# A six-layer cross network on one core: another way to load and transpose the last 32 features of x0

## The chip, the core and the metric

The kernel runs on one NeuronCore of a Trainium2 chip. The core has five instruction streams: TensorE (PE in the profile; PEld is its weight load), VectorE (DVE), ScalarE (ACT), GpSimd (POOL) and SyncE (SP, which only issues transfers here). ScalarE issues transfers too. A transfer (DMA) runs on the core's 16 DMA engines. The metric is device microseconds of one execution; shorter is better. Most executions of one kernel agree within 0.3%.

## The reference

x0 is 4096 x 416, ws is 6 x 416 x 416, bs is 6 x 416, all bfloat16.

```python
def reference(x0, ws, bs):
    x = x0
    for l in range(ws.shape[0]):
        x = x0 * (x @ ws[l] + bs[l]) + x
    return x
```

## The kernel before, in words

The 416 features are cut into NK = 3 groups of 128, the main part, and a remainder of R = 32. For layers 0 to 4 the activations lie transposed, features on partitions: `XM[i]` holds the main part (128 partitions, 3 groups, 4096 columns of batch), `XR[i]` the remainder. The batch is cut in NS = 2 halves of 2048 and each half in NG = 4 blocks of CW = 512. The remainder would fill only 32 partitions, so the four blocks of a half are stacked: partition 32g + r of `XR` is feature 384 + r of block g, and `XR` has 512 columns per half. `XM[0]` and `XR[0]` hold x0 and are read in every layer. `XRd` is a copy of `XR[0]` with its upper and lower 64 partitions exchanged; only layer 0 reads it.

**The loads.** `load_x0t(s, g)` (L75) loads one of the eight x0 blocks, main part, 512 rows, through a transposing DMA on SyncE's queue. `load_wm(eng, l)` (L71) loads a layer's main weights, `load_wr0` (L87) the remainder rows of layer 0's weights to 32 partitions of `WR`, which L108 (ScalarE, twice) and L110 (GpSimd) copy to the other three groups of 32. Layer 0's main weights, the biases (`bsb`, L100), the remainder of half 0 and `load_wr0` are issued by ScalarE in this order, followed by a dummy activation on `dz` (L104) that brings the load of the activation table with it. A transfer is also held back at its issue until the transfer that had its completion semaphore before has landed; there are eight such semaphores, given out in turn.

**The remainder of x0** reaches `XR[0]` in three steps. For half 0, `load_xrem0` (L80) issues four transfers on ScalarE's queue, each for every fourth tile of 128 rows, so that a row of `xrig[:, 0, i]` holds the 32 remainder features of four batch rows side by side. For half 1, `load_xrem1` (L84) is one transfer on SyncE's queue to `xrem`, after the fifth x0 block, and GpSimd (L132) rearranges `xrem` to `xrig[:, 1]`. Then `x0_rem(s, tpr)` (L153) transposes four 128x128 tiles on TensorE (L155) into PSUM, and VectorE copies the result to `XR[0]` and, in two exchanged halves, to `XRd` (L158).

**Layer 0** (`first_layer`, L206) runs half by half. `full` (L212) multiplies the three main groups of one block, `row` (L219) adds the remainder's product; for the output group m = 1 it reads `XRd`. `mm_rem` (L191, L196) makes the 32 remainder outputs. In half 0 the order on TensorE is: nine `full` matmuls of block 0, the four remainder transposes, nine of block 1, eight `row` matmuls, eighteen for blocks 2 and 3, four `row`, `mm_rem`, the four transposes for half 1. Each PSUM result goes through ScalarE, which adds the bias (L163, L171), and VectorE, which multiplies by x0 (L164, L172) and adds x (L167, L173). PSUM is a pool of four tiles of two banks each; the transposes of half 0 take a tile of their own, those of half 1 the second bank of the remainder tile `pr`.

**Layers 1 to 4** use the same parts with matmuls of 32 output columns (L179, L185), and the last layer works with batch on partitions (L325 to L353) and stores the output. While the first transfers are under way, TensorE runs filler matmuls (L139).

A scheduler orders the instructions of each engine by its own estimates; an instruction given to `tc.keep_in_program_order` keeps its place on its engine in the order of the program.

Of the kernel before, what the change touches and what calls it, by code (L numbers as in the profile page):

```python
# [9 lines left out]
ACT = mybir.ActivationFunctionType  # L10
ALU = mybir.AluOpType
BF16 = mybir.dt.bfloat16
# [4 lines left out]
def kernel(  # L17
# [7 lines left out]
    nc = tc.nc  # L25
    B, D = x0.shape
    L = ws.shape[0]
    P = 128
    NK = 3
    R = D - NK * P  # L30
    assert R == 32 and B == 4096 and D == 416 and L >= 2
    NS = 2
    NG = 4
    CW = 512
    SW = NG * CW
# [4 lines left out]
    big = ctx.enter_context(tc.tile_pool(name="big", bufs=1))  # L40
    tpool = ctx.enter_context(tc.tile_pool(name="tpool", bufs=6))
    opool = ctx.enter_context(tc.tile_pool(name="opool", bufs=10))
    psum = ctx.enter_context(tc.tile_pool(name="psum", bufs=4, space=bass.MemoryType.PSUM))

    x0_v = x0.rearrange("(bt p) d -> p bt d", p=P)
    out_v = out.rearrange("(bt p) d -> p bt d", p=P)

    ident = const.tile([P, P], BF16)
    dz = const.tile([P, 2], FP32)
    ones = const.tile([P, P], BF16)  # L50
    WM = const.tile([P, L, NK, D], BF16)
    WR = const.tile([P, L, D], BF16)
# [3 lines left out]
    bM = const.tile([P, NK, L], FP32)  # L56
    bR = const.tile([P, L], FP32)
    X0rows = big.tile([P, NBT, D], BF16)
    XLrows = big.tile([P, NBT, D], BF16)
    scrR = [big.tile([P, 4, P], BF16, name=f"scrR{s}") for s in range(NS)]  # L60
    xrem = big.tile([P, 16, R], BF16)
    xrig = big.tile([P, NS, 4, P], BF16)
    XRd = big.tile([P, NS * CW], BF16)
    XM = [big.tile([P, NK, B], BF16, name=f"XM{i}") for i in range(3)]
    XR = [big.tile([P, NS * CW], BF16, name=f"XR{i}") for i in range(3)]

    def col0(s, g):
        return SW * s + CW * g
# [4 lines left out]
    def load_x0t(s, g):  # L73
        c0 = col0(s, g)
        nc.sync.dma_start_transpose(out=XM[0][:, :, c0:c0 + CW], in_=x0[c0:c0 + CW, 0:NK * P])  # L75

    def load_xrem0():
        with nc.allow_non_contiguous_dma(reason="64B row segments"):
            for i in range(4):
                nc.scalar.dma_start(xrig[:, 0, i, :].rearrange("p (g r) -> p g r", g=NG), x0_v[:, i:16:4, NK * P:D])  # L80

    def load_xrem1():
        with nc.allow_non_contiguous_dma(reason="64B row segments"):
            nc.sync.dma_start(xrem[:], x0_v[:, 16:32, NK * P:D])  # L84

    def load_wr0():
        nc.scalar.dma_start(WR[0:R, 0, :], ws[0, NK * P:D, :])  # L87

    def load_wr(eng, g, l0, l1):
        eng.dma_start(WR[32 * g:32 * g + 32, l0:l1, :], ws[l0:l1, NK * P:D, :].rearrange("l r n -> r l n"))  # L90
# [8 lines left out]
    load_wm(nc.scalar, 0)  # L99
    nc.scalar.dma_start(bsb[:], bs[:, :])  # L100
    load_x0t(0, 1)
    load_xrem0()
    load_wr0()
    nc.scalar.activation(dz[:, 1:2], dz[:, 0:1], ACT.Identity, bias=dz[:, 0:1], scale=1.0)  # L104
    for g in range(1, NG):
        dst, src = WR[32 * g:32 * g + 32, 0, :], WR[0:R, 0, :]
        if g < NG - 1:
            nc.scalar.copy(dst, src)  # L108
        else:
            nc.gpsimd.tensor_copy(dst, src)  # L110
    for g in range(2, NG):
        load_x0t(0, g)
    load_x0t(1, 0)
    load_xrem1()
    for g in range(1, NG):
        load_x0t(1, g)
    load_wm(nc.sync, 1)
    for g in range(NG):
# [8 lines left out]
    def fill_wd(l0, l1):  # L127
        for g in range(NG):
            nc.gpsimd.tensor_copy(WD[32 * g:32 * g + 32, l0:l1, g, :], WR[32 * g:32 * g + 32, l0:l1, NK * P:D])

    fill_wd(0, 1)
    nc.gpsimd.tensor_copy(xrig[:, 1].rearrange("p i (g r) -> p i g r", g=NG), xrem[:].rearrange("p (g i) r -> p i g r", g=NG))  # L132
    fill_wd(1, L)

    wps = psum.tile([P, CW], FP32, tag="ps", name="wps")
# [8 lines left out]
    def bias_setup():  # L144
        pb = psum.tile([P, 4, 8], BF16, tag="ps", name="pb")
        for m in range(NK):
            nc.tensor.transpose(pb[:, m, 0:L], bsb[0:L, 128 * m:128 * m + 128], ident[0:L, 0:L])
        for g in range(NG):
            nc.tensor.transpose(pb[32 * g:32 * g + 32, 3, 0:L], bsb[0:L, NK * P:D], ident[0:L, 0:L], tile_position=(0, 32 * g))  # L149
        nc.vector.tensor_copy(bM[:], pb[:, 0:NK, 0:L])  # L150
        nc.vector.tensor_copy(bR[:], pb[:, 3, 0:L])

    def x0_rem(s, tpr):  # L153
        for i in range(4):
            nc.tensor.transpose(tpr[:, 128 * i:128 * i + 128], xrig[:, s, i, :], ident[:])  # L155
        for dst, src in ((slice(0, P), slice(0, P)), (slice(64, P), slice(0, 64)), (slice(0, 64), slice(64, P))):
            to = XR[0] if dst == src else XRd
            nc.vector.tensor_copy(to[dst, CW * s:CW * s + CW], tpr[src])  # L158

    def ew_main(l, s, m, h, pt, cur, nxt, pin=False):  # L160
        c0 = col0(s, 2 * h)
        t = tpool.tile([P, 2 * CW], BF16, name="t")
        nc.scalar.activation(t[:], pt[:].rearrange("p a b -> p (a b)"), ACT.Identity, bias=bM[:, m, l:l + 1], scale=1.0)  # L163
        prod = nc.vector.tensor_tensor(out=t[:], in0=t[:], in1=XM[0][:, m, c0:c0 + 2 * CW], op=ALU.mult)  # L164
        if pin:
            tc.keep_in_program_order(prod)
        nc.vector.tensor_tensor(out=nxt[:, m, c0:c0 + 2 * CW], in0=t[:], in1=cur[:, m, c0:c0 + 2 * CW], op=ALU.add)  # L167

    def ew_rem(l, s, pr, curR, nxtR):
        tr = tpool.tile([P, 2 * CW], BF16, name="t")  # L170
        nc.scalar.activation(tr[:, 0:CW], pr, ACT.Identity, bias=bR[:, l:l + 1], scale=1.0)  # L171
        nc.vector.tensor_tensor(out=tr[:, 0:CW], in0=tr[:, 0:CW], in1=XR[0][:, CW * s:CW * s + CW], op=ALU.mult)  # L172
        nc.vector.tensor_tensor(out=nxtR[:, CW * s:CW * s + CW], in0=tr[:, 0:CW], in1=curR[:, CW * s:CW * s + CW], op=ALU.add)  # L173
# [15 lines left out]
    def mm_rem(l, s, pr, cur, curR):  # L189
        for g in range(NG):  # L190
            nc.tensor.matmul(pr[32 * g:32 * g + 32, :], lhsT=WD[:, l, g, :], rhs=curR[:, CW * s:CW * s + CW],  # L191
                             start=True, stop=False, tile_position=(0, 32 * g))
        for k in range(NK):
            for g in range(NG):
                c0 = col0(s, g)
                nc.tensor.matmul(pr[32 * g:32 * g + 32, :], lhsT=WM[:, l, k, NK * P:D], rhs=cur[:, k, c0:c0 + CW],  # L196
                      start=False, stop=(k == NK - 1), tile_position=(0, 32 * g))
# [8 lines left out]
    def first_layer(s):  # L206
        cur, curR, nxt, nxtR = XM[0], XR[0], XM[1], XR[1]

        def full(pt, m, h, gl, after_row):
            c0 = col0(s, 2 * h + gl)  # L210
            for k in range(NK):
                nc.tensor.matmul(pt[:, gl, :], lhsT=WM[:, 0, k, 128 * m:128 * m + 128], rhs=cur[:, k, c0:c0 + CW],  # L212
                                 start=(k == 0 and not after_row), stop=(k == NK - 1 and after_row))

        def row(pt, m, h, opens):
            for gl in range(2):
                rg = 32 * ((2 * h + gl) ^ (2 if m == 1 else 0))
                src = XRd if m == 1 else curR
                nc.tensor.matmul(pt[:, gl, :], lhsT=WR[rg:rg + 32, 0, 128 * m:128 * m + 128],  # L219
                                 rhs=src[rg:rg + 32, CW * s:CW * s + CW],  # L220
                                 start=opens, stop=not opens, tile_position=(rg, 0))

        def ph(m):
            return psum.tile([P, 2, CW], FP32, tag="ps", name=f"ph{m}")

        pa = [ph(m) for m in range(NK)]
        if s == 0:
            for m in range(NK):
                full(pa[m], m, 0, 0, False)
            tp0 = psum.tile([P, CW], BF16, tag="ps", name="tpr")  # L230
            x0_rem(0, tp0[:])
            for m in range(NK):
                full(pa[m], m, 0, 1, False)
        else:
            for m in range(NK):
                for gl in range(2):
                    full(pa[m], m, 0, gl, False)
        pb = [ph(0)]
        row(pa[0], 0, 0, False)
        row(pb[0], 0, 1, True)  # L240
        row(pa[2], 2, 0, False)
        row(pa[1], 1, 0, False)
        for m in range(NK):
            ew_main(0, s, m, 0, pa[m], cur, nxt)
        for m in range(NK):
            if m:
                pb.append(ph(m))
            for gl in range(2):
                full(pb[m], m, 1, gl, m == 0)
        row(pb[1], 1, 1, False)  # L250
        row(pb[2], 2, 1, False)
        pr = psum.tile([P, 2, CW], FP32, tag="ps", name="pr")
        mm_rem(0, s, pr[:, 0, :], cur, curR)
        if s == 0:
            x0_rem(1, pr[:, 1, :].bitcast(BF16)[:, 0:CW])
        for m in range(NK):
            ew_main(0, s, m, 1, pb[m], cur, nxt, pin=(s == 0))
        ew_rem(0, s, pr[:, 0, :], curR, nxtR)

    bias_setup()  # L260
    pe_filler(1, CW)
    for s in range(NS):
        first_layer(s)
# [147 lines left out]
```

## Time and profile before

| | us |
|---|---|
| median of three runs (lowest to highest) | 130.73 (130.52 to 130.84) |
| the profiled execution | 130.58 |
| its span, first to last instruction | 128.8 |
| TensorE busy | 123.6 |
| VectorE busy | 106.7 |
| ScalarE busy | 86.9 |
| GpSimd busy | 6.2 |

| first 17 us of the profiled execution | starts at | takes |
|---|---|---|
| table load on ScalarE (L104) | 6.00 | 1.28 |
| nine `full` matmuls, block 0 | 5.91 | 2.16 |
| nine `full` matmuls, block 1 | 8.63 | 2.09 |
| copy to `XR[0]`, half 0 (L158) | 8.67 | 0.42 |
| two copies to `XRd`, half 0 (L158) | 9.13 | 0.86 |
| first eight `row` matmuls | 10.73 | 0.69 |
| GpSimd's rearranging copy (L132) | 15.00 | 1.06 |

Times inside the profile count from the first instruction of the span. The page names a group of instructions by its source line, its engine and out<-in. The chain of waits follows the work that ended last back through whatever released it; its pieces add up to the span. A line with ACTq or SPq is the issue of a transfer, not the transfer; the DMA views give the time from issue to landing. Differences under some tenths of a microsecond inside one profile are real for that execution, but one execution differs from the next by up to 0.3%.

### The profile page before, as it was taken

What the parts mean: (1) busy time and instruction counts of PE and PEld (TensorE: products, weight loads), DVE (VectorE), ACT (ScalarE), POOL (GpSimd) and SP (SyncE); (2) the same over time, 40 slices, a digit from 0 to 9 for tenths busy, and PEclk for the clock granted to TensorE, in tenths of its full rate; (3) what the DMA queues carried; (4) which work ended last, traced back from release to release, by engine and by line L of the source; (5) the groups of instructions that cost most, each with busy time, mean ns of one, the idle gap of its engine ahead of it and who ended that gap; (6) DMA issues with size and microseconds to landing.
All of it is one profiled execution on the core that took longest, in us unless ns stands there. A gap on an engine that the chain in (4) does not pass through costs nothing.

```text
span 128.8 us, 3973 instructions
## 1 busy us (share of the span) xinstructions
PE 123.6 (96%) x1691; PEld 55.1 (43%) x1691; DVE 106.7 (83%) x195; ACT 86.9 (67%) x99; POOL 6.2 (5%) x18
## 2 busy tenths in 40 slices
PE   7999999999999999999999999999999999999960
PEld 3343443344545444434444544444444445445420
DVE  0023989999999898989898989898989899898991
ACT  0138873887848667848668848668858896569670
POOL 4004300600000000000000000000000000000000
PEclk9999999999999999999999999999999999999999
DMA  4999999999990000000000000000297999985754
GB/s 95 244 231 207 163 153 264 253 328 333 336 291 9 5 0 8 0 0 5 0 5 0 5 0 5 0 5 0 45 163 169 119 237 191 217 261 186 235 178 138
DMA packets 42102, 16.37 MB, mean 127 GB/s; under 512 B 30906, under 2 KB 42084, under 8 KB 42084
## 3 DMA queue, kind: packets, MB, share of 16 engines
q1 hardware_dynamic: 39368, 15.53, 53.9%
q10 hardware_dynamic: 2716, 0.59, 2.5%
q8 instruction: 13, 0.21, 0.7%
q14 instruction: 5, 0.04, 0.1%
HBM read 6.15 MB, written 3.41 MB: 74 GB/s over the span
## 4 chain that ended last, share of the span: by engine, by line
PE 89%; DVE 6%; issue 2%; ACT 1%; DVEq 0%
PE pt L179 49%; PE ph L212 13%; PE py L325 8%; PE pt L185 5%; PE pr L196 5%; PE wps L139 4%; DVE t L353 4%; DVE o L342 2%; PE pr L191 2%; PE ph L219 1%; PE py L331 1%; PE py L334 1%; ACT t L352 1%; PE tpr L155 0%; PE pr L155 0%
## 5 line engine op out<-in xcount | busy, mean ns | idle before, releaser
L179 PE MATMUL pt<-XM,WM 128*32 128x512 bf16 x1152 | 65.2, 379 | 0.0
L163 ACT ACTIVATE t<-pt,bM 128x1024 bf16<-128x1024 f32 x48 | 49.6, 1115 | 18.5 <-PE pt L185 18.5
L164 DVE TENSOR_TENSOR t<-t,XM 128x1024 bf16<-128x1024 bf16 x60 | 41.4, 690 | 5.2 <-ACT t L163 5.2
L167 DVE TENSOR_TENSOR XM<-t,XM 128x1024 bf16<-128x1024 bf16 x60 | 41.8, 697 | 3.4
L179 PEld LDWEIGHTS <-WM 128*32 128x32 bf16 x1152 | 29.7, 97 | 33.8 <-issue 5.1
L352 ACT CAST t<-py 128x416 bf16<-128x416 f32 (+1 forms) x23 | 14.8, 642 | 4.8 <-PE py L325 2.6
L325 PE MATMUL py<-WM,XM 128*128 128x416 bf16 x96 | 17.7, 340 | 0.0
L212 PE MATMUL ph<-XM,WM 128*128 128x512 bf16 x72 | 16.5, 381 | 0.0
L163 ACT ACTIVATE t<-ph,bM 128x1024 bf16<-128x1024 f32 x12 | 12.5, 1114 | 3.4 <-PE ph L219 3.4
L325 PEld LDWEIGHTS <-XM 128*128 128x128 bf16 x96 | 9.0, 98 | 8.5 <-issue 1.4
L353 DVE TENSOR_TENSOR t<-t,X0rows 128x416 bf16<-128x416 bf16 (+1 forms) x23 | 10.4, 457 | 1.2 <-ACT t L352 1.2
L342 DVE TENSOR_TENSOR o<-t,XLrows 128x416 bf16<-128x416 bf16 (+1 forms) x23 | 10.4, 456 | 0.0
L212 PEld LDWEIGHTS <-WM 128*128 128x128 bf16 x72 | 6.7, 98 | 8.4 <-issue 1.1
L171 ACT ACTIVATE t<-pr,bR 128x512 bf16<-128x512 f32 x10 | 6.4, 685 | 2.7 <-PE pr L196 2.1
L196 PE MATMUL pr<-XM,WM 128*32 128x512 bf16 x120 | 8.2, 379 | 0.0
L185 PE MATMUL pt<-XR,WR 32*128 32x512 bf16 x96 | 7.3, 379 | 0.0
L139 PE MATMUL wps<-const-bfloat16-1.0 128*128 128x512 bf16 (+1 forms) x12 | 4.9, 592 | 0.8 <-PEq L395 0.8
L104 ACT ACT_TABLE_LOAD x1 | 1.3, 1283 | 6.0 <-DMA XM<-in_x_dram 6.0
L173 DVE TENSOR_TENSOR XR<-t,XR 128x512 bf16<-128x512 bf16 x10 | 4.2, 425 | 0.7
L196 PEld LDWEIGHTS <-WM 128*32 128x32 bf16 x120 | 3.2, 97 | 3.0
L150 DVE CAST bM<-pb 128x18 f32<-128x18 bf16 x1 | 0.2, 177 | 5.1 <-PE pb L149 5.1
L172 DVE TENSOR_TENSOR t<-t,XR 128x512 bf16<-128x512 bf16 x10 | 4.2, 420 | 0.0
(38 smaller groups left out, 33.5 us busy)
## 6 DMA issues: line engine op xcount, KB each, us to landing
X0rows<-in_x_dram SPq DMA_DIRECT2D x4, 832.0 KB, 11.5
out_dram<-o SPq DMA_DIRECT2D x9, 208.0 KB, 2.5
WM<-in_ws_dram SPq DMA_DIRECT2D x5, 312.0 KB
out_dram<-o SPq DMA_DIRECT2D x13, 104.0 KB, 1.9
WR<-in_ws_dram SPq DMA_DIRECT2D x4, 130.0 KB, 4.1
WM<-in_ws_dram ACTq DMA_DIRECT2D x1, 312.0 KB
XM<-in_x_dram SPq DMA_TRANSPOSE x8, 4.9
xrig<-in_x_dram ACTq DMA_DIRECT2D x4, 32.0 KB, 4.2
```

Source lines behind the costliest of these rows:

```text
L139: nc.tensor.matmul(wps[:, 0:cols], lhsT=warm[:, 0:P], rhs=warm[:, 0:cols], start=True, stop=True)
L163: nc.scalar.activation(t[:], pt[:].rearrange("p a b -> p (a b)"), ACT.Identity, bias=bM[:, m, l:l + 1], scale=1.0)
L164: prod = nc.vector.tensor_tensor(out=t[:], in0=t[:], in1=XM[0][:, m, c0:c0 + 2 * CW], op=ALU.mult)
L167: nc.vector.tensor_tensor(out=nxt[:, m, c0:c0 + 2 * CW], in0=t[:], in1=cur[:, m, c0:c0 + 2 * CW], op=ALU.add)
L179: nc.tensor.matmul(pts[g // 2][32 * q:32 * q + 32, g % 2, :], lhsT=WM[:, l, k, 128 * m + 32 * q:128 * m + 32 * q + 32], rhs=cur[:, k, c0:c ...
L185: nc.tensor.matmul(pts[g // 2][:, g % 2, :], lhsT=WR[32 * g:32 * g + 32, l, 128 * m:128 * m + 128], rhs=curR[32 * g:32 * g + 32, CW * s:CW ...
L196: nc.tensor.matmul(pr[32 * g:32 * g + 32, :], lhsT=WM[:, l, k, NK * P:D], rhs=cur[:, k, c0:c0 + CW], start=False, stop=(k == NK - 1), tile ...
L212: nc.tensor.matmul(pt[:, gl, :], lhsT=WM[:, 0, k, 128 * m:128 * m + 128], rhs=cur[:, k, c0:c0 + CW], start=(k == 0 and not after_row), sto ...
L325: nc.tensor.matmul(py[:, 0:D], lhsT=cur[:, k, q_cols(q, g)], rhs=WM[:, l, k, :], start=((not closes) and k == 0), stop=(closes and k == NK ...
L342: tc.keep_in_program_order(nc.vector.tensor_tensor(out=o, in0=t, in1=xl, op=ALU.add))
L352: nc.scalar.copy(tv, src)
L353: tc.keep_in_program_order(nc.vector.tensor_tensor(out=tv, in0=tv, in1=X0rows[:, b, :], op=ALU.mult))
```

## The change

The remainder of a half is now loaded by one transfer that puts 16 consecutive batch rows on each partition: partition p, slot t of `xrem[s]` is row 2048 s + 16 p + t. VectorE's transpose instruction transposes each 32x32 block (32 partitions by the 32 features of one slot); its output is written in steps of 16 columns, so that batch row 16 j + t of a block comes to stand in column 16 j + t of `XR[0]`, as before. `XRd` is copied from `XR[0]` in SBUF, no longer from PSUM. `xrig`, GpSimd's rearranging copy, the eight transposes on TensorE and the PSUM tile for them are gone.

Both remainder loads are on ScalarE's queue: the first behind the table load, the dummy activation and `load_wr0`, the second behind ScalarE's two copies of `WR`. The table load moves up to follow the bias load. SyncE's queue has the eight x0 blocks in a row. The new order on ScalarE and the order of VectorE's bias and remainder steps are kept in program order (`pin`). TensorE runs the nine matmuls of block 0 and the nine of block 1 with nothing between them.

```diff
-    xrem = big.tile([P, 16, R], BF16)
-    xrig = big.tile([P, NS, 4, P], BF16)
+    xrem = [big.tile([P, 16, R], BF16, name=f"xrem{s}") for s in range(NS)]
...
-    def load_xrem0():
-        with nc.allow_non_contiguous_dma(reason="64B row segments"):
-            for i in range(4):
-                nc.scalar.dma_start(xrig[:, 0, i, :].rearrange("p (g r) -> p g r", g=NG), x0_v[:, i:16:4, NK * P:D])
-
-    def load_xrem1():
-        with nc.allow_non_contiguous_dma(reason="64B row segments"):
-            nc.sync.dma_start(xrem[:], x0_v[:, 16:32, NK * P:D])
+    def pin(ins):
+        tc.keep_in_program_order(ins)
+
+    def load_xrem(s):
+        with nc.allow_non_contiguous_dma(reason="64B row segments"):
+            pin(nc.scalar.dma_start(xrem[s][:], x0[SW * s:SW * s + SW, NK * P:D].rearrange("(p t) r -> p t r", p=P)))
 
     def load_wr0():
-        nc.scalar.dma_start(WR[0:R, 0, :], ws[0, NK * P:D, :])
+        pin(nc.scalar.dma_start(WR[0:R, 0, :], ws[0, NK * P:D, :]))
...
     load_x0t(0, 1)
-    load_xrem0()
+    pin(nc.scalar.activation(dz[:, 1:2], dz[:, 0:1], ACT.Identity, bias=dz[:, 0:1], scale=1.0))
     load_wr0()
-    nc.scalar.activation(dz[:, 1:2], dz[:, 0:1], ACT.Identity, bias=dz[:, 0:1], scale=1.0)
+    load_xrem(0)
     for g in range(1, NG):
         dst, src = WR[32 * g:32 * g + 32, 0, :], WR[0:R, 0, :]
         if g < NG - 1:
-            nc.scalar.copy(dst, src)
+            pin(nc.scalar.copy(dst, src))
         else:
             nc.gpsimd.tensor_copy(dst, src)
+    load_xrem(1)
     for g in range(2, NG):
         load_x0t(0, g)
-    load_x0t(1, 0)
-    load_xrem1()
-    for g in range(1, NG):
+    for g in range(NG):
         load_x0t(1, g)
...
-    nc.gpsimd.tensor_copy(xrig[:, 1].rearrange("p i (g r) -> p i g r", g=NG), xrem[:].rearrange("p (g i) r -> p i g r", g=NG))
...
-        nc.vector.tensor_copy(bM[:], pb[:, 0:NK, 0:L])
-        nc.vector.tensor_copy(bR[:], pb[:, 3, 0:L])
-
-    def x0_rem(s, tpr):
-        for i in range(4):
-            nc.tensor.transpose(tpr[:, 128 * i:128 * i + 128], xrig[:, s, i, :], ident[:])
-        for dst, src in ((slice(0, P), slice(0, P)), (slice(64, P), slice(0, 64)), (slice(0, 64), slice(64, P))):
-            to = XR[0] if dst == src else XRd
-            nc.vector.tensor_copy(to[dst, CW * s:CW * s + CW], tpr[src])
+        pin(nc.vector.tensor_copy(bM[:], pb[:, 0:NK, 0:L]))
+        pin(nc.vector.tensor_copy(bR[:], pb[:, 3, 0:L]))
+
+    def x0_rem(s):
+        cs = slice(CW * s, CW * s + CW)
+        pin(nc.vector.transpose(XR[0][:, cs].rearrange("p (j t) -> p t j", t=16), xrem[s][:]))
+        for dst, src in ((slice(64, P), slice(0, 64)), (slice(0, 64), slice(64, P))):
+            pin(nc.vector.tensor_copy(XRd[dst, cs], XR[0][src, cs]))
...
         if s == 0:
-            for m in range(NK):
-                full(pa[m], m, 0, 0, False)
-            tp0 = psum.tile([P, CW], BF16, tag="ps", name="tpr")
-            x0_rem(0, tp0[:])
-            for m in range(NK):
-                full(pa[m], m, 0, 1, False)
+            x0_rem(0)
+            for gl in range(2):
+                for m in range(NK):
+                    full(pa[m], m, 0, gl, False)
...
         if s == 0:
-            x0_rem(1, pr[:, 1, :].bitcast(BF16)[:, 0:CW])
+            x0_rem(1)
```

## The prediction

> **What bounds the kernel now.** I read the page first: who is busy.
>
> ```profile
> PE 123.6 (96%) x1691; PEld 55.1 (43%) x1691; DVE 106.7 (83%) x195; ACT 86.9 (67%) x99; POOL 6.2 (5%) x18
> PEclk9999999999999999999999999999999999999999
> ```
>
> TensorE is busy for 123.6 of 128.8 us at full clock, so a microsecond is won only where TensorE waits or does work that can leave it. Everything that the diff touches lies before 18.4 us, so next I read the chain of waits for 5 to 22 us (start, length, what).
>
> ```profile
> 5.91 2.16 PE ph L212 x9
> 8.07 0.33 PE tpr L155 x3
> 8.40 0.00 issue
> 8.40 0.23 PE tpr L155
> 8.63 2.09 PE ph L212 x9
> 10.73 0.69 PE ph L219 x8
> 11.42 3.99 PE ph L212 x18
> ...
> 16.06 0.65 PE pr L196 x12
> 16.71 0.33 PE pr L155 x4
> 17.04 3.88 PE ph L212 x18
> 20.93 0.54 PE ph L219 x8
> ```
>
> The chain is all TensorE. Three places are of interest: 8.07 to 8.63, where four remainder transposes stand between the first two x0 blocks; the row block at 10.73, 0.15 us longer than its twin at 20.93; and the four transposes at 16.71. What do they wait for? The timeline of ScalarE (start, length) and the DMA view of the second x0 block, issued at 2.2:
>
> ```profile
> 1.90 2.48 ACTq L80 DMA_DIRECT2D xrig<-in_x_dram  x4
> 5.64 0.34 ACTq L87 DMA_DIRECT2D WR<-in_ws_dram  x1
> 6.00 1.28 ACT L104 ACT_TABLE_LOAD   x1 [6.00 <-DMA XM<-in_x_dram]
> 9.66 1.10 ACT L108 COPY WR<-WR 32x416 bf16<-32x416 bf16 x2 [2.07 <-DMA WR<-in_ws_dram]
> ```
>
> ```profile
> XM<-in_x_dram SPq DMA_TRANSPOSE x1, 6.4
> ```
>
> Issued at 2.17, landed 6.4 us later: 8.57. So the matmuls at 8.63 waited for their block, and the transposes merely fill that wait. To take them out gains nothing unless this block lands earlier. The DMA view by microsecond (6 to 7, then 9 to 10) says why it is late:
>
> ```profile
> q1 hardware_dynamic: 742, 0.19, 85.4%
> q10 hardware_dynamic: 752, 0.05, 52.5%
> ```
> ```profile
> q1 hardware_dynamic: 1144, 0.28, 128.2%
> ```
>
> q1 is SyncE's queue (the blocks), q10 ScalarE's (the remainder's 64-byte pieces). Beside q10 the block moves 742 packets in a microsecond; alone, 1144.
>
> **The change, part by part.**
>
> *ScalarE's queue.* The bias issue ends at 1.18 + 0.69 = 1.87. The table load (1.28) and the dummy activation (0.29) now follow and end at 3.47, then WR's issue (0.34) to 3.8, then the first remainder load (0.59, SyncE's row for the same 128 KB) from 3.85 to 4.4. Before, WR's issue stood at 5.64 because its completion semaphore was still held by the first x0 block; in the new order neither load waits. WR lands 4.0 after its issue (its row), at 7.5; ScalarE's two copies end at 8.6 instead of 10.76. That last end is why the first row block took 0.69 and not 0.54: 0.15 us won.
>
> *Second x0 block.* No remainder packet comes ahead of it now. 393 KB are 1536 packets of 256 bytes; at 1144 per us they need 1.34 us, and they took about 2.5. I need 0.5 us of that: with a landing by 8.07 the eighteen matmuls run on without a break. Eighteen cost 3.99 (row at 11.42), so nine cost 2.00, and the row block starts at 8.07 + 2.00 = 10.06 instead of 10.73: 0.67 won.
>
> *First remainder.* Loads of this kind took 4.2 us (a quarter, ScalarE) and 4.6 us (all 128 KB, SyncE, L84). With the last quarter, issued at 4.0 and waited for until 8.17, that is 8.0 to 9.1 for one issued at 3.85; I take 8.75. The VectorE transposition is in no row of this trace. From below, the 128x512 copy at L158: 0.42. From above, GpSimd's rearranging copy of the same 128x512 at L132: 1.06. VectorE's two sizes (0.69 at 1024 columns, 0.42 at 512) give 0.53 ns a column plus 0.15 fixed; the output goes out in steps of 16 elements, so I double the rate term: 0.69, ready at 9.44. The two XRd copies now read SBUF: at most 0.42 each (L158), at least 0.18 (L150, 18 columns); I take 0.3, ready at 10.05. TensorE needs XR0 at 10.06 and XRd some 0.4 later. No wait in the middle; at the bad ends (9.1, 1.06, 0.42 twice) XRd is ready at 11.0 and TensorE waits 0.55. These VectorE instructions lie in its idle stretch before 12.2, so they cost nothing else.
>
> A rule weighs against me here: the Trainium skill, "VectorE: DVE Perf Modes", section "The three transpose paths", gives 311 ns for 128x128 bf16 on VectorE, and 390 ns on TensorE. Four such would make 1.24 us (an estimate from that page), XRd ready at 10.6 and a wait of 0.15, so 129.85 by that figure; no run here shows it yet.
>
> *Row block and after.* It ends at 10.06 + 0.54 = 10.60 instead of 11.42. The third x0 block is then wanted at 10.6 (before: 11.4) and the fourth three matmuls later, at 11.27 (before: 12.1). By the trace's semaphore records they landed at 9.8 and 11.5. Same bytes, same engines: I see no reason for the fourth to come much sooner, so TensorE may wait 0 to 0.24 there; I take 0.12 off.
>
> *Second remainder.* Removed: SyncE's issue (0.58), GpSimd's copy (1.06), four TensorE transposes (0.33 on the chain, and the 18 matmuls that follow are ready), and VectorE's 0.48 wait for them. GpSimd's was cover only: its next fill waited for WR until 23.0 anyway. Added: an issue on ScalarE behind the two WR copies, at 8.6; nothing but the evictions from about 10.2 stands behind it. Landing at 8.6 + 4.6 = 13.2; VectorE wants it at about 15.6, after the first half's three products and sums. 0.33 won. VectorE's transposition and copies (1.3) stand where three copies (1.28) stood, and end a good microsecond earlier than 18.39. SyncE's later blocks move up by 0.6 and more, against a TensorE that moves up by 1.0: the eighth landed at 21.2 and was wanted at 22.1, so it keeps its margin.
>
> *Sum.* 0.67 + 0.15 + 0.33 - 0.12 = 1.03 us. From 18 us on the chain is TensorE without a wait until the last layer, whose VectorE tail starts from TensorE's results: it all slides. The profiled run took 130.58 (span 128.8 and 1.8 around it): 129.55. The median shown is 0.15 higher: 129.7.
>
> **The rivals.**
>
> *A, the first remainder is late (slower).* One 128 KB load on ScalarE's queue, issued at 3.85, comes through beside the third block instead of the second. Break-even: the row block must end 0.33 later than it did (11.75), so XRd ready at 11.4, so a landing near 10.0, 6.2 us after issue. For: the second block itself took 6.4 beside this very traffic. Against: the four quarters took 4.2 to 5.1 each by the semaphore records, under that traffic. Each microsecond later is one lost; a landing at 11.8 would give 131.5. Chance 0.10.
>
> *B, the gap moves to the fourth x0 block.* The remainder's packets now stand ahead of blocks three and four. If they push the fourth to 12.0, TensorE waits 0.73 at 11.27: 130.3. For: the DMA row is at 9 in each of the first slices, so bytes moved off one block fall on another. Against: before, all of this was ahead of the fourth block too. The Trainium skill, "DMA: Bandwidth & Descriptors", section "Issuing engines are not separate DMA queues", says that transfers of all issuers share the same 16 engines and only issue time is saved; the two counts of q1 above agree. Chance 0.15.
>
> *C, the transposition is slow.* At 1.5 us and 0.42 a copy, XRd is ready at 11.1 and TensorE waits 0.65: 130.35. For: no row of it. Against: no VectorE row here costs over 1 us. Chance 0.08.
>
> *D, the change doesn't do what it says for the second block.* If its slow landing is its own and not q10's, TensorE still starts at 8.6; only 0.15 and 0.33 are won: 130.2. Against: 742 against 1144. Chance 0.07.
>
> **How the numbers follow.** The forecast has 0.60 and spans 129.4 (no wait at the fourth block, and 0.15 us of scatter) to 130.1 (0.4 of waits). A measurement here tells about 0.3% (0.4 us) from no change, that is, below 130.34 is faster. The forecast, most of B, all of D and half of C are: 0.60 + 0.11 + 0.07 + 0.04, cut to 0.79 for what I have not seen. Slower (above 131.1): 0.09 from A. Same: the rest, 0.12. The range takes in B, C and D: 129.4 to 130.6.
>
> **What would show it.** In the profile after: no L155; the eighteen first matmuls unbroken from 5.9 to 10.1; the row block at about 10.1 with 0.54; the table load near 1.9; the remainder load landing under 5.1 us after its issue; the transposition between 0.42 and 1.06; 18 matmuls straight after the rem block at about 15.7. I am wrong if TensorE's idle time before L213 (the rows) names VectorE, or if the wait stands ahead of the third or fourth block's matmuls.

## The result, and the profile after

| | before | after |
|---|---|---|
| median (lowest to highest), us | 130.52 (130.42 to 130.84) | 130.93 (130.77 to 131.28) |
| ratio of the times, 95% interval | | 1.003 (1.0019 to 1.0041) |
| profiled execution, its span, us | 130.58, 128.8 | 130.93, 129.1 |

The change makes the kernel 0.4 us slower; 1 us faster was forecast, 129.7. (The three runs of before ahead of the prediction had a median of 130.73; the nine here have 130.52.) The page of after, first row and the row of the transposition (count, busy, mean ns, then idle time and what ended it):

```profile
PE 123.1 (95%) x1681; PEld 54.8 (42%) x1683; DVE 109.7 (85%) x195; ACT 86.8 (67%) x99; POOL 5.1 (4%) x17
L150 DVE STREAM_TRANSPOSE XR<-xrem 128x512 bf16<-128x512 bf16 x2 | 4.7, 2364 | 2.1 <-DMA xrem<-in_x_dram 2.1
```

TensorE lost 0.5 us of work, as wanted, but the span grew by 0.3. The chain of waits of after, 5 to 22 us:

```profile
4.86 1.55 SPq L74
6.42 0.04 issue
6.46 5.86 DMA XM<-in_x_dram
12.32 0.04 issue
12.36 0.38 PE ph L206
12.74 0.05 issue
12.79 2.97 PE ph L206 x13
15.76 0.33 PE ph L213 x4
16.09 0.33 PE pr L185 x4
16.42 0.65 PE pr L190 x12
17.06 3.56 PE ph L206 x16
20.62 0.05 issue
20.68 0.38 PE ph L206
21.06 0.54 PE ph L213 x8
```

Before, this stretch was TensorE alone. Now a transfer stands in it: the fourth x0 block, issued at 6.46, landed at 12.32 (before: 11.51), and TensorE waited for it. So a row at 21.06 replaces one at 20.93. (The two pieces of 0.05 called issue each stand where the trace lacks the record of one of 18 matmuls; they are no waits.) TensorE's own timeline of after shows what came first (the square bracket is the wait and what ended it):

```profile
5.84 2.38 PE L206 MATMUL ph<-XM,WM 128*128 128x512 bf16 x9
8.63 2.10 PE L206 MATMUL ph<-XM,WM 128*128 128x512 bf16 x9 [0.41 <-DMA XM<-in_x_dram]
10.75 0.61 PE L213 MATMUL ph<-XR,WR 32*128 32x512 bf16 x6
11.40 1.77 PE L206 MATMUL ph<-XM,WM 128*128 128x512 bf16 x5
```

The second block starts at 8.63, exactly where it started before: with the four transposes gone TensorE is idle in that gap. ScalarE's timeline tells why:

```profile
1.91 1.28 ACT L99 ACT_TABLE_LOAD   x1 [1.91 <-issue]
1.98 0.32 ACTq L84 DMA_DIRECT2D WR<-in_ws_dram  x1
2.33 0.64 ACTq L81 DMA_DIRECT2D xrem<-in_x_dram  x1
5.81 0.54 ACT L105 COPY WR<-WR 32x416 bf16<-32x416 bf16 x1 [2.31 <-DMA WR<-in_ws_dram]
5.82 0.55 ACTq L81 DMA_DIRECT2D xrem<-in_x_dram  x1
```

The loads behind the table load in program order were issued at 1.98 and 2.33, while it ran (1.91 to 3.19); the second remainder load went out at 5.82, as the first of the two `WR` copies began. So the time that an instruction runs did not hold up the transfer behind it, but the copy's own wait for `WR` (landed 5.79) did: the only semaphore that this load needed was free from 5.57. The DMA views of after for 6 to 7 us, where the second block is read, and then for 9 to 10 us, where the fourth is due:

```profile
q10 hardware_dynamic: 1267, 0.08, 87.1%
q1 hardware_dynamic: 497, 0.13, 55.9%
```
```profile
q10 hardware_dynamic: 2062, 0.13, 141.6%
q1 hardware_dynamic: 121, 0.02, 11.8%
```

Before, the blocks' queue (q1) moved 742 packets in the first of these microseconds and 1144 in the second; now it moves 497 and 121, since 64-byte pieces of the remainder (q10) take the engines in both. VectorE, with its first remainder step:

```profile
8.35 2.35 DVE L150 STREAM_TRANSPOSE XR<-xrem 128x512 bf16<-128x512 bf16 x1 [2.14 <-DMA xrem<-in_x_dram]
10.74 0.61 DVE L152 COPY XRd<-XR 64x512 bf16<-64x512 bf16 x2
```

The transposition took 2.35 us, not 0.69, and ended at 10.70. So even a second block at 8.07 would not have brought the rows ahead of 10.7.

The loss up to the rows of half 1 is 0.13 us (21.06 against 20.93), and it stays 0.13 until the last VectorE step (126.03 against 125.90). The spans differ by 0.31. The rest is in the closing waits of SyncE, of which the semaphore records of the traces tell. The waits by line (total, times, longest), first before, then after:

```profile
SPq L406 <- DMA out_dram<-o: 1.4, 4, 0.5
```
```profile
SPq L398 <- DMA out_dram<-o: 1.6, 2, 1.4
```

At the end SyncE checks the eight completion semaphores in a fixed row of five waits. Before, the last store landed at 127.97 under the semaphore checked last, and the row ended at once, at 127.98. The change has three transfers fewer, the semaphores are given out in turn, and so the last store came under the second: landed 128.09, then three more waits, 0.065 us apart, the last at 128.30. That is 0.2 us.

### The profile page after: what moved, and what is told of

Same layout as the page of the kernel before. It is cut to its first block, busy times and chain, and to the rows that moved or that the text cites. A ratio compares the mean times of both kernels' runs of the same rounds, so it can differ in the third digit from the quotient of the medians.

```text
span 129.1 us, 3949 instructions
## 1 busy us (share of the span) xinstructions
PE 123.1 (95%) x1681; PEld 54.8 (42%) x1683; DVE 109.7 (85%) x195; ACT 86.8 (67%) x99; POOL 5.1 (4%) x17
## 4 chain that ended last, share of the span: by engine, by line
PE 80%; DVE 5%; DMA 5%; SPq 4%; issue 2%; ACT 1%; DVEq 0%
PE pt L173 49%; PE ph L206 9%; PE py L317 8%; PE pt L179 5%; PE pr L190 5%; DMA XM<-in_x_dram 5%; SPq L74 4%; DVE t L345 3%; DVE o L334 2%; PE pr L185 2%; PE py L323 1%; PE ph L213 1%; PE py L326 1%; ACT t L344 1%; DVEq L398 0%
## 5 line engine op out<-in xcount | busy, mean ns | idle before, releaser
L150 DVE STREAM_TRANSPOSE XR<-xrem 128x512 bf16<-128x512 bf16 x2 | 4.7, 2364 | 2.1 <-DMA xrem<-in_x_dram 2.1
```

## The experiments

Two theories stand against each other. By the one (Q in the expectations) the packets of the remainder loads decide which x0 block comes late. By the other (D, or D2 for the fourth block) the blocks are late by themselves. E is the theory that the place of the last store's semaphore in the closing row costs 0.2 us, and W that layer 1's weights delay the eighth block.

To take the end of the kernel out of a comparison, some kernels below get tiny transfers of a row of biases, 832 bytes each, to unused partitions, so that the last store meets the closing row as in before.

**The end.** Two runs for the closing waits: after with three tiny transfers, and before with five.

```diff
+    for g in range(3):      # before: range(5)
+        nc.sync.dma_start(bLr[8 * g + 1:8 * g + 2, :], bs[LL:LL + 1, :])
```

> The changed kernel with three more tiny transfers (rows of the last layer's bias to unused partitions of bLr, behind the four that are there, some 50 us before anything waits on SyncE). The kernel closes with SyncE waiting for its completion semaphores in a fixed order, two to an instruction of 0.065 us. The change issues three transfers fewer, so the last store got the semaphore that stands second in that row instead of last, and three waits follow its landing. Theory E (end of kernel): with three transfers more the last store has the last semaphore again, the closing part shrinks by 0.19 us, and the time falls to 130.74. Rival: the end is scatter of the stores, the time stays at 130.93.

> The kernel before with five more such tiny transfers, so that its last store gets the semaphore that stands second in the closing row, as in the changed kernel. Theory E: the kernel before becomes slower by 0.19 us, to 130.76, with nothing else touched. Rival: it stays at 130.57.

After fell to 130.74 (130.63 to 131.05), before rose from 130.56 to 130.75 (ratio 1.0011, 1.0002 to 1.0019). The price is 0.19 us, shown in both directions, and it was not won at the start (in the profile of the first run the second and fourth block landed at 8.72 and 12.45, 0.13 later than in after). Without it the change costs 0.18 us: 130.74 against 130.56 (ratio 1.0011, 1.0000 to 1.0021, so hardly clear of the noise).

**The transposition.** Written densely; the remainder's columns then come in another order than the main part's, so the output isn't the reference's.

```diff
-        pin(nc.vector.transpose(XR[0][:, cs].rearrange("p (j t) -> p t j", t=16), xrem[s][:]))
+        pin(nc.vector.transpose(XR[0][:, cs].rearrange("p (t j) -> p t j", t=16), xrem[s][:]))
```

> The VectorE transposition writes its output densely, block after block, so XR[0] holds each block's columns in another order; loads and order untouched. If the step of 16 columns in its output is what makes it slow, it takes 0.6 to 1.3 us instead of 2.35; if the transposition itself is slow, it stays at 2.3. In both cases theory Q says that the first row block stays at about 10.7, because the second x0 block lands at 8.6, and the time stays within 0.15 us of the changed kernel's 130.93. Rival T (the slow transposition is what ate the gain): the time falls by 0.5 us or more.

VectorE's timeline of that run:

```profile
8.43 0.71 DVE L150 STREAM_TRANSPOSE XR<-xrem 128x512 bf16<-128x512 bf16 x1 [3.07 <-DMA xrem<-in_x_dram]
```

0.71 us instead of 2.35: the steps of 16 columns cost 1.64 us. The time stayed, 130.98 (130.78 to 131.39), for the second block landed at 8.67 and the fourth at 12.40. Only the row block gained: 0.55 (10.74 to 11.29) instead of 0.65, since `XRd` was ready when it began. The slow transposition lay just behind the late block.

**Is it the remainder that makes the blocks late?** The first load left out (`xrem[0]` is filled with zeros by GpSimd), and the same with the end made equal by four tiny transfers.

```diff
-    load_xrem(0)
+    nc.gpsimd.memset(xrem[0][:], 0.0)
```

> The first remainder load is left out; a memset on GpSimd fills xrem of half 0 instead. Theory Q: with no remainder packets beside it the second x0 block lands by 8.0 instead of 8.59, the eighteen first matmuls run unbroken, the row block starts at about 10.1, the fourth block lands before 11.6, and the time falls by 0.7 to 1.0 us, to about 130.0. Rival D: the second block lands at 8.5 or later all the same and at most 0.35 us is won.

> Without the first remainder load (memset on GpSimd), now with four tiny transfers more so that the last store has the last semaphore. By theory E 0.26 us less than the run without them, 130.86. Its profile is a second look at why most executions of that kernel took 131.1 while the profiled one took 130.48: if the second block lands near 7.1 and TensorE runs unbroken to the row block at 10.2 again, the loss lies later, and the chain names the place.

The second block landed at 7.07 and 6.95 instead of 8.59, and the 18 matmuls ran unbroken. The times were 131.12 (130.48 to 131.5; the profiled execution is the lowest) and 130.82 (130.43 to 131.45): nothing won. TensorE's timeline of the second run:

```profile
9.82 0.60 PE L215 MATMUL ph<-XR,WR 32*128 32x512 bf16 x6
10.36 0.82 PE L208 MATMUL ph<-XM,WM 128*128 128x512 bf16 x3
12.27 1.02 PE L208 MATMUL ph<-XM,WM 128*128 128x512 bf16 x4 [1.09 <-DMA XM<-in_x_dram]
```

The rows came 0.9 us earlier, and the whole of it was lost three matmuls later: the fourth block, with the second remainder load's packets beside it from 8.26 to 11.43, landed only at 12.23. That is the prediction's rival B; how much of it is the remainder's doing, the run without any remainder traffic below tells. (This execution, 130.64, is 0.18 under the median, so where the typical one loses time is not shown.)

**The second load back on SyncE**, behind the fifth block as in before; then the same with layer 1's main weights held until the eighth block has landed, three tiny transfers and one of GpSimd's fills of `WD` moved ahead (these two are not shown below).

```diff
-    load_xrem(1)
...
+    load_x0t(1, 0)
+    load_xrem(1, nc.sync)
+    for g in range(1, NG):
         load_x0t(1, g)
+    nc.gpsimd.tensor_copy(WM[0:1, 1, 0, 0:1], XM[0][0:1, 0, B - 1:B])   # second run only
     load_wm(nc.sync, 1)
```

> The second remainder load goes back to SyncE's queue behind the fifth x0 block, all else as in the changed kernel. Theory Q (ScalarE's sequencer issues loads while the table load still runs, so both remainder loads start some 2 us sooner than I had reckoned and their packets delay the x0 blocks beside them): the fourth x0 block lands at 11.6 or before instead of 12.32, TensorE no longer waits ahead of the eighteen matmuls, and the time falls by about 0.35 us, to 130.6. Rival D (a block's landing is set by its own transfer, not by the remainder): the fourth block stays at 12.3 and the time at 130.9.

> The second remainder load back on SyncE as in the earlier run of that name; layer 1's main weights wait until the eighth x0 block has landed (GpSimd copies one element of it into the weights' tile first); and three tiny transfers more, for the last store's semaphore. Theory W (the packets queued right behind a block hold back its completion: in that earlier run the eighth block's last packet came at 19.95 and its landing at 22.09): the eighth block lands by 21.0, TensorE doesn't wait for it at 21.9, what the fourth block's earlier landing won is kept, and the time is 130.3 to 130.4, below the kernel before. Rival (the eighth block's own transfer is late): it lands at 22 and the time is 130.7.

The fourth block landed at 11.25 and TensorE did not wait there. But the time was 130.89 (ratio 1.0026, 1.0016 to 1.0036). The chain of waits of the first run:

```profile
15.77 6.32 DMA XM<-in_x_dram
22.09 0.04 issue
22.13 1.89 PE ph L207 x8
```

The eighth block landed at 22.09 (before: 21.16), a little after it was wanted: the gain at the fourth block was given back there. Holding the weights did not help: 22.18, and 130.69 (130.56 to 130.93), no more below the first run than the three tiny transfers in it are worth. But SyncE's timeline of that run shows that it did not free the place behind the block:

```profile
17.95 1.06 SPq L87 DMA_DIRECT2D WR<-in_ws_dram  x2
22.88 0.41 SPq L70 DMA_DIRECT2D WM<-in_ws_dram  x1
```

Two loads of the later layers' remainder weights moved up and were issued right behind the eighth block, where the main weights had stood. So layer 1's main weights are not needed for the delay, but the wider form of theory W, that packets queued right behind a block hold back its landing, is not tested. Why the block lands some 2 us after its last packet is read (20.16 in that run) stays open.

**Both loads later on ScalarE's queue.** A one-column activation that writes into the load's target stands ahead of each load, so that the issue must wait for it.

```diff
+    pin(nc.scalar.activation(xrem[0][:, 0, 0:1], dz[:, 0:1], ACT.Identity, bias=dz[:, 0:1], scale=1.0))
     load_xrem(0)
...
+    pin(nc.scalar.activation(xrem[1][:, 0, 0:1], XM[0][:, 0, CW:CW + 1], ACT.Identity, bias=dz[:, 0:1], scale=1.0))
     load_xrem(1)
```

> Each remainder load is made to wait for a one-column activation on ScalarE that writes its tile first: the first for one behind the table load and the dummy activation, the second for one that reads the second x0 block. So the first is issued at about 3.7, as the prediction had it, the second at about 8.7. Theory Q: the second block lands by 8.1 and the fourth by 11.6. But the first remainder then lands at 8.5 to 9.1 and the 2.35 us transposition ends at about 11.2, so the row block starts at 11.2 instead of 10.75 and the time is 130.8 to 131.2. If the transposition didn't bind it would be 130.0. Rival D: second block at 8.6, fourth at 12.3 as in the changed kernel, time 131.3.

The first load went out at 3.71, about where the prediction put it, and the second block still landed at 8.60. Its last packet was read at 6.41; the remainder's packets followed from 6.37 to 7.34 and landed at 8.63, together with it. Each block's data, 1536 packets of 256 bytes, is followed by 32 packets of 4 bytes, which by their place and size close it. The DMA view of this run for 7.05 to 7.2 us has 28 of them:

```profile
q10 hardware_dynamic: 318, 0.02, 145.8%
q1 hardware_dynamic: 28, 0.00, 10.5%
```

So the remainder's pieces (1429 packets of q10 from 6.3 to 7.03) had come between the block's data and its closing packets. The transposition then ran until 11.07, the rows waited for it (0.37 us, released by VectorE), and the time was 131.31 (ratio 1.0056, 1.0041 to 1.0071), 0.38 above after. So the prediction's order on ScalarE, even had it come about, would not have moved the second block.

**The second load held, or left out.** First after with the second load alone held until the second block has landed (the second added line above), and three tiny transfers. Then after without that load (zeros from GpSimd), and four.

> The kernel after, with the second remainder load held on ScalarE's queue until the second x0 block has landed (a one-column activation that reads that block stands ahead of its issue), and three tiny transfers added so that the closing waits meet the last store as in the kernel before. Theory Q (the remainder's packets decide which block comes late: issued at 5.8, the second load delays the fourth block): issue at about 8.9, its packets at 11 to 12.5 and so behind the fourth block; the fourth block lands at 11.0 to 11.5 instead of 12.32, no wait of TensorE there, rows at 10.75 still, the 18 matmuls after the remainder's 32 outputs at about 16.7 instead of 17.06; the eighth block lands at about 21.4, no wait. Total 130.3 to 130.4, below the kernel before. Rival B2 (what is taken from the fourth block is paid by a later one, as where this load stood behind the fifth block): the eighth block lands at 22 or later, 130.6 to 130.75.

> The kernel after without the second remainder load (the remainder of half 1 is filled with zeros by GpSimd instead), and four tiny transfers added so that the closing waits meet the last store as in the kernel before. Theory Q: the fourth block lands at 11.5 or earlier, no wait of TensorE there, the second block still at 8.6 and rows at 10.75; half 1 starts at about 16.7; total 130.3 to 130.4. Theory D2 (the fourth block comes late by itself, since all blocks follow each other on SyncE's queue): it lands at 12.2 to 12.4 as after, the wait of 0.3 stays, 130.7.

The chain of waits of the run with the load held:

```profile
8.72 2.10 PE ph L209 x9
10.82 0.02 issue
10.84 0.71 PE ph L216 x8
11.55 0.97 PE ph L209 x4
12.52 0.05 issue
12.57 2.97 PE ph L209 x13
```

Issued at 9.03, the load left the fourth block alone: landed at 11.01, no wait, and the eighth came in time (21.13). 130.50 (130.38 to 130.67): 0.24 us better than after with the same end (130.74), and level with before (ratio 0.9993, 0.9981 to 1.0005). Leaving the load out gave hardly more, 130.47 (130.3 to 130.53), with the fourth block at 11.18. So the second load's early issue costs after 0.24 us; the expectations' 130.3 to 130.4 was 0.1 too low.

**No remainder traffic at all.** Both loads replaced by zeros from GpSimd, five tiny transfers.

> The kernel after without either remainder load (both remainders are filled with zeros by GpSimd), and five tiny transfers added so that the closing waits meet the last store as in the kernel before. This measures what the whole traffic of the remainder costs. Theory Q: the second block lands at 7.0 as without the first load, the fourth at 11.0 or earlier, so neither wait is left: 18 matmuls unbroken, rows at about 10.0, half 1 at about 16.0; total about 129.6, the sum of the prediction. Theory D2 (the blocks are late by themselves): TensorE waits at the fourth block until 12 or later; total 130.3 or more.

TensorE's timeline of that run:

```profile
5.71 4.04 PE L208 MATMUL ph<-XM,WM 128*128 128x512 bf16 x18 [0.51 <-DMA XM<-in_x_dram]
9.69 0.60 PE L215 MATMUL ph<-XR,WR 32*128 32x512 bf16 x6
10.23 0.82 PE L208 MATMUL ph<-XM,WM 128*128 128x512 bf16 x3
11.72 1.46 PE L208 MATMUL ph<-XM,WM 128*128 128x512 bf16 x5 [0.67 <-DMA XM<-in_x_dram]
```

129.94 (129.88 to 130.24), 0.62 us under before. The rows came at 9.69, but the fourth block, with nothing beside it but the other blocks, landed at 11.68 and took 0.67 back (the profiled execution, 130.24, is the slowest of its six). So both theories hold in part: the second block is late through the remainder, the fourth waits even without it. That is no fixed floor, for with the first load in and the second held it had landed at 11.01; here its last data packet was read at 10.21, and what kept it until 11.68 stays open. Even without a single remainder packet the forecast's 129.7 is not reached.

**Is anything left to win at the second block?** The run with the second load held, with the first load behind three activations, the dense transposition (columns in another order, as above), and the second load behind four activations more.

```diff
+    for i in range(3):
+        pin(nc.scalar.activation(xrem[0][:, 0, 0:1], dz[:, 0:1], ACT.Identity, bias=dz[:, 0:1], scale=1.0))
     load_xrem(0)
```

> The kernel of the run with the second load held back, with three more changes. The first remainder load waits on ScalarE's queue behind three one-column activations (issue about 4.3 instead of 2.33, its packets then from about 6.9, some 0.4 after the last packet of the second x0 block, which without remainder traffic is read at 6.46). The transposition is written densely (0.71 instead of 2.35; the columns of the remainder then come in another order than those of the main part, so the output isn't the reference's). The second load waits for four activations more. It asks whether anything is left to win at the second block. Theory T (only packets that are read before or together with a block's delay it): the block lands at 7.0 to 7.6, the load at about 9.0, XR[0] ready at about 9.8, rows at about 10.2 instead of 10.84, the fourth block lands between 11 and 12 and is wanted at 11.7; total 130.0 to 130.3. Theory U (a block's landing also waits for the packets that follow it closely, as with the issue at 3.71): the block lands at 8.5 or later, rows at 10.8 or later; total 130.5 to 130.8.

TensorE's timeline of that run:

```profile
5.71 4.04 PE L213 MATMUL ph<-XM,WM 128*128 128x512 bf16 x18 [0.56 <-DMA XM<-in_x_dram]
10.35 0.60 PE L220 MATMUL ph<-XR,WR 32*128 32x512 bf16 x6 [0.60 <-DVE XR L157]
11.00 2.21 PE L213 MATMUL ph<-XM,WM 128*128 128x512 bf16 x9
```

Issued at 4.37, the load let the second block land at 7.21; it landed itself at 9.48, and the rows waited for VectorE until 10.35, 0.4 earlier than before. This execution took 130.26, but the twelve ranged from 129.84 to 131.32 (median 130.48, ratio 0.9997, 0.9974 to 1.0021). In the profile theory T is right; in the time nothing is shown. The first remainder packet was read at 6.42 here and at 6.37 in the run issued at 3.71, and the block landed 1.4 us apart: the order of these two transfers stands on an edge. Here the block's 32 closing packets went at 6.41 to 6.52, ahead of nearly all of the remainder (112 packets of q10 from 6.4 to 6.53).

## Why the prediction was wrong

*ScalarE's queue* (WR's issue at 3.5, the first remainder load from 3.85, the second at 8.6): wrong. The table load and the dummy activation ahead of the transfers did not hold their issue; the rows show 1.98, 2.33 and 5.82. This put the second load's packets ahead of the fourth block (0.24 us); for the second block an issue at 3.85 would not have helped, as the run issued at 3.71 shows. The prediction read before's order (issue, then table load) as a queue in which each waits for the one ahead. But before's table load itself began only at 6.00, after the issues, so that row said nothing of the reverse.

*Second block, 0.67.* Nothing was won. "No remainder packet comes ahead of it now" failed: 1267 of them moved beside it in 6 to 7 us. The cause named was right, since without the first load the block lands 1.5 us earlier; the outcome of rival D came about, but not its reason. And the step was built too simply: it counted packets ahead of the block's data, but in the run issued at 3.71 the remainder's pieces passed between the data (read by 6.41) and the closing packets (7.06 to 7.34), and the block landed at 8.60. The Trainium skill, "DMA: Bandwidth & Descriptors", section "Queues, rings and completion order", says that a completion increment lands only after every earlier write of that DMA engine, across its queues. Both runs agree, if the closing packets carry the increments, which the traces do not say: issued at 3.71, most of the remainder went ahead of them, and block and remainder landed together at 8.60 and 8.63; issued at 4.37, nearly all of it went behind them, and the block landed at 7.21 with the remainder read until 8.96.

*First remainder's load, landed by 8.75 (4.2 to 5.1 us after its issue).* It took 6.0 (2.33 to 8.33). That it landed before 8.75 was luck: it was issued 1.5 us sooner than reckoned. The prediction also misread its own rows in small ways: the last quarter was waited for until 8.40, not 8.17, and the second block's packets took 2.1 us (4.90 to 6.98), not about 2.5. Neither changes the outcome.

*Row block, 0.15.* 0.04 came (0.65 instead of 0.69). `WR` landed at 5.79 and was no longer late, so the mechanism was right; `XRd`, through the transposition, gave it back: the half that these rows read was ready only at 11.03, and they read it from 11.08. With the dense one it took 0.55.

*Transposition, 0.69 (0.42 to 1.06).* 2.35: the term mis-sized most, and outside its bounds. Without the fixed 0.15 that the prediction used, the dense one leaves 0.56 for 512 columns, not the 0.27 of a copy, and the strided one 2.20, not 0.54: the transposition itself was underrated by two, and its steps cost a factor of four, not two. The upper bound came from GpSimd, an engine that says nothing of VectorE's strided writes. The figure that the prediction weighed from the Trainium skill, "VectorE: DVE Perf Modes", section "The three transpose paths" (an estimate of 1.24 for four tiles), is too high for the dense form and too low for this one. The Trainium skill, "SBUF — State Buffer", section "Door 1: The DMA port swizzle", says that accesses which cross to a new 16-byte line each time pay a penalty, for bf16 from a step of more than 8; the step here is 16, and the two runs agree with it. It moved the end little only because the second block was late as well: XR[0] at 10.70, the second block's last matmul at 10.73.

*Fourth block, 0 to 0.24 of wait.* About 0.3 (the matmul was due at 12.06 and began at 12.36), the very sign that the prediction named for being wrong. The prediction let the second load in at 8.6; at 5.82 its packets filled 9 to 10 us. Holding it took the wait away and 0.24 us with it. This is rival B in mild form; without the first load the wait was 1.09, and 0.67 even with no remainder at all.

*Transposes of half 1, 0.33.* Mostly right: from the start of the remainder's 32 outputs to the rows of half 1 it took 4.87 us before (16.06 to 20.93) and 4.64 after (16.42 to 21.06), so 0.23. VectorE's 3 us more (109.7 against 106.7) hid behind TensorE; the prediction had reckoned with next to none, so this was margin and not foresight.

*"It all slides."* True to the last store (0.13 at 21.06, 0.13 at 126.03), false behind it: 0.19 for the place of its semaphore. The prediction counted transfers for their time but not for the turn in which semaphores are given out.

The sum, then: forecast 0.67 + 0.15 + 0.33 - 0.12 = 1.03 won. In the profile: -0.02 up to the rows, 0.04 for the row block, -0.38 from there to the remainder's outputs, with the fourth block's wait (5.02 against 4.64), 0.23 for the transposes, -0.18 at the end: -0.31, the difference of the spans.

## What to carry to other kernels

A transfer's place in the program is not its place in time. Here the time that an instruction ran (the table load's 1.28) held back no transfer behind it; what did was the instruction's own wait (the `WR` copy, 5.81, and the load behind it, 5.82) or the transfer's need of its result (the activations put in). So look for what each issue waits for, then ask whose bytes it will travel beside. When a stage has several loads and one set of DMA engines, taking bytes off one block's way puts them on another's; cost the whole row of landings against the times at which they are wanted, not one landing. And a VectorE instruction that no row shows should be costed from a row of its own engine with the same access steps, or measured alone first.

## What the runs showed of the hardware

- A transposition of 32x32 blocks on VectorE, 128x512 bf16, took 0.71 us written densely and 2.35 us written in steps of 16 elements.
- ScalarE issued transfers at 1.98 and 2.33 while its table load ran from 1.91 to 3.19; a transfer behind a copy that waited until 5.81 was issued at 5.82.
- A transfer's landing can come long after its last packet is read: 6.41 and 8.60 for the second block with the remainder close behind it, 6.50 and 7.21 with the remainder issued 0.66 us later. In the first case the block's 32 packets of 4 bytes went at 7.06 to 7.34, in the second at 6.41 to 6.52.
- 2048 pieces of 64 bytes nearly filled the 16 DMA engines for about a microsecond in after (2062 packets from 9 to 10 us, 0.13 MB), in which the x0 blocks moved 121 packets (1144 there in before).
- The number of transfers in a kernel decides which of the closing waits meets the last store, and that was worth 0.19 us.
